# Sequence table scaled ahead of W1's issues and rounded behind them, and a last product in two column halves, in a fused attention, Fourier mixing and MLP kernel

## The chip, the cores and the metric

The kernel runs on one core of a Trainium2 chip. The metric is device time of one execution in microseconds (us); lower is better. The engines are named as in the profile: PE is TensorE, DVE is VectorE, ACT is ScalarE, POOL is GpSimd, SP is SyncE.

## The reference

Shapes: `q`, `k`, `v` are (8, 12, 448, 64), `w_ch1` is (768, 3072), `w_ch2` is (3072, 768), all float32; the output is (8, 448, 768).

```
scores = (q @ k.T) / sqrt(64);  attn = relu(scores)**2 / 448
x  = heads merged (attn @ v)                        # (8, 448, 768)
u  = x + real(fft(fft(x, over the sequence), over the channels))
un = (u - mean(u)) / sqrt(var(u) + 1e-6)            # over the channels
out = u + relu(un @ w_ch1) @ w_ch2
```

## The kernel before

**Work and stages.** Eight batches are taken one after the other. In a batch, four groups of three heads give scores on PE (L954), relu on ACT (L967), the square on DVE (L984) and the product with v on PE (L822, L827); its result, x transposed, is copied into `xT` (L671, L673, L689). The Fourier transform is two products with cosine and sine tables: over the channels (L1407, its result copied as `pc` by L1451), then over the 448 sequence positions (L1029), where x itself is added through an identity or a reversing matrix (L1032). Rows are normalised and turned (L1130, L1146), and two MLP products follow with weights that stay in on-chip memory; most of the MLP is formed on sums and differences of blocks (`Pair`), so that fewer products are needed.

**The first batch is special.** Its attention runs while the tables are still being made. Symmetric channels are first added and subtracted (`fold`, L748), on DVE, between the squares. The sequence table `seq` is made by `seq_table` on GpSimd: index numbers (L358, L360), scaled to turns in two pieces (L363, L366), rounded by adding and taking off 1.5*2^23 (L369), and the rounded part taken off (L371). Then `seq_sines` takes an absolute value on DVE (L377) and three sines on ACT (L383). Behind these ACT loads another function table (L399) and copies its half of `pc` (L1451); DVE copies the other half. The first batch's row products are eight: `rows(t, hf)` for four tiles t of 112 or 128 rows and two halves hf of 384 columns (L1029, L1032); the tiles 0 to 2 take banks of the pool `psS`, and `rows(3, 0)` and `rows(3, 1)` take one bank each of `psF`, a pool of two. Transposes of the next batch's q and k (`turn_on_pe`, L623) also take a bank of `psF`, which comes free when ACT or DVE has copied it into `qkT` (L630).

**What sets the order.** Everything is written as generators. Each step of one says `yield need(engine, duration, dependencies, banks)`, and a planner (`Streams.run`) picks at compile time, with these estimated durations, the step that could start first; equal ones go by a rank that `sch.add(generator, rank)` gives, lower first. So each engine's order is fixed in the program, an engine does its instructions strictly in that order, and a changed estimate or rank can move instructions anywhere. GpSimd issues the loads, in the order of the generator `loading`: `load_group(i, which, parts)` loads q (0), k (1) or v (2) of group i, `parts` 0 being the first 384 positions and 1 the last 64 (`load_halves`, L451); `load_w1` issues six pieces of W1 (L515); `mirrors`, called inside `load_group(NG + 1, ...)`, builds the reversing matrices and the index lists.

**The end.** The last product of the last pair (`Pair.chain_a`, its last step) is 12 matmuls into a 128x384 tile (L2060); DVE adds it to the residual `o` (L1616), and SP stores `o` (L1596).

Of the kernel before, what the change touches and what calls it, by code (L numbers as in the profile page):

```python
# [161 lines left out]
def dve(n):  # L162
    return n / 960 + 0.15
# [14 lines left out]
def kernel(  # L178
# [174 lines left out]
    def seq_table():  # L353

        f = work.tile([128, 4 * KH], FP32, name="dfty", tag="uA", bufs=1)
        g = work.tile([128, 4 * KH], FP32, name="dfty", tag="uB", bufs=1)
        yield need("POOL", 0.55)
        nc.gpsimd.iota(drow[:, 0:2], pattern=[[128, 2]], base=0, channel_multiplier=1,  # L358
                       allow_small_or_imprecise_dtypes=True)
        nc.gpsimd.iota(dcol[:, 0:SX], pattern=[[1, SX]], base=0, channel_multiplier=0,  # L360
                       allow_small_or_imprecise_dtypes=True)
        yield need("POOL", 0.3)
        nc.gpsimd.tensor_scalar(drow[:, 0:2], drow[:, 0:2], 1.0 / S, None, op0=ALU.mult)  # L363
        for i in range(2):
            yield need("POOL", 0.45)
            nc.gpsimd.tensor_scalar(f[:, i * SX:(i + 1) * SX], dcol[:, 0:SX], drow[:, i:i + 1], None, op0=ALU.mult)  # L366
        f, g = f[:, 0:2 * SX], g[:, 0:2 * SX]
        yield need("POOL", 0.75)
        nc.gpsimd.tensor_scalar(g, f, ROUND, -ROUND, op0=ALU.add, op1=ALU.add)  # L369
        e = yield need("POOL", 1.1)  # L370
        nc.gpsimd.tensor_tensor(f, f, g, op=ALU.subtract)  # L371
        sch.add(seq_sines(f, g, e + LATENCY["POOL"]), (0, 0.3))

    def seq_sines(f, g, e):

# [7 lines left out]
            nc.scalar.activation(dst, y, AF.Sin, bias=bias, scale=sign * 2.0 * math.pi)  # L383
        seq_ready.t = nseq_ready.t = dft_ready.t = e + LATENCY["ACT"]

    ROUND = 1.5 * 2 ** 23
    chan_made, dft_made = [Cell() for _ in range(3)], Cell()

# [67 lines left out]
    def load_group(i, which=(0, 1, 2), parts=(0, 1)):  # L456

        b, g = divmod(i, NG)
        hs = slice(g * HG, (g + 1) * HG)
        for x, src in enumerate((q, k, v)):  # L460
            if x not in which:
                continue
            if 0 in parts:
                if b == 0 and x < 2:
                    e = yield need("POOL", 0.75, ring())
                    t = first_qk[x][:R, g] if x == 0 else first_qk[x][:, g]
                else:
# [8 lines left out]
                nc.gpsimd.dma_start(out=to, in_=src[b, hs, 0:rows].rearrange("h (p j) d -> p h (j d)", j=j))  # L476
                loads[i][x] = None if x == 2 else t.rearrange("p h (j d) -> p j h d", j=4)
                landed.append(sch.dma(e, GRP * rows / S, 390e3, "sw"))
                arrive(i, x)
            if i == 0 and x == 1:  # L480
                e = yield need("POOL", 0.55)
                dft_indices()
                indices_ready.t = e + LATENCY["POOL"]
                yield need("POOL", 0.6)
                make_identity(nc, ident)
            if x and 1 in parts and (b > 0 or g == x - 1):
                yield from load_halves(b, g if b else 0, 1 if b else NG, x)
            if i == 2 and x == 2:
                yield need("POOL", 0.75)
                pads()  # L490
            if i == NG + 1 and x == 1 and 0 in parts:
                yield need("POOL", 3.6)
                mirrors()


    qk_left = Cell()
# [35 lines left out]
    def loading():  # L532
        for i in range(NG):
            yield from load_group(i)

        yield from load_group(NG, (0, 1))
        yield from load_group(NG + 1, (0, 1), (0,))
        yield from load_w1(0)
        yield from seq_table()
        yield from load_group(NG + 1, (1,), (1,))  # L540
        yield from load_w1(1)
        for i in (NG, NG + 1):
            yield from load_group(i, (2,), (0,))
# [1010 lines left out]
    def uses():  # L1554
# [11 lines left out]
                at += [(g, c, 0, 0), (g, c + 1, 0, 1 + odd), (g, c + 1, 1, 3 + odd), (g, c, 1, 5)]  # L1566
        return at

    os, ot, added = {}, {}, {}
    for g, c, hf, _ in uses():  # L1570
        ot[g, c, hf], added[g, c, hf] = Cell(), Cell()

    def outputs(slot):

        for g, c, hf, at in uses():
# [19 lines left out]
            e = yield need("SP", 0.1, [added[g, c, hf]])  # L1595
            nc.sync.dma_start(out=rows[t0:t0 + 128, cs], in_=o)  # L1596
            e = sch.dma(e, 128 * DH * 4)
            yield need("SP", 0.0, [e])

    def ffns():  # L1600
# [6 lines left out]
    def adder(b, NC, pool):  # L1607
# [4 lines left out]
        def add(pc, e, c, hf, give=True):  # L1612

            e = yield need("DVE", dve(DH), [e + LATENCY["PE"], ot[b, c, hf]])
            o = os[b, c, hf]
            nc.vector.tensor_tensor(o, pc[:, 0:DH], o, op=ALU.add)  # L1616
            if give:
                pool.give(pc, e)
            left[c, hf] -= 1
# [388 lines left out]
    class Pair:  # L2008
# [4 lines left out]
        def __init__(self, b, c, at, ht, add, advance, pieces, pool):  # L2013
# [3 lines left out]
            self.r12, self.r4 = ([Cell() for _ in pieces] for _ in range(2))  # L2017
            self.m1, self.m2, self.done = Cell(), Cell(), [Cell(), Cell()]
            self.reads = Cell(), Cell()
            self.waits, Pair.read = Pair.read, [self.reads[0], self.reads[1], *self.r4]  # L2020

        def early(self):
# [34 lines left out]
        def product(self, pc, lhs, rhs, start, i0=0, i1=KP):  # L2057

            for i in range(i0, i1):
                nc.tensor.matmul(pc[:, 0:DH], lhsT=lhs[i], rhs=rhs[i], start=(start and i == 0),  # L2060
                                 stop=(i == KP - 1), skip_group_check=True)
            self.advance((i1 - i0) * mm(DH))

        def first(self, k):

# [21 lines left out]
        def chain_a(self):  # L2087
# [111 lines left out]
```

## Time and profile before

| | |
|---|---|
| Runs | 571.01, 571.33, 572.6 us; median 571.33 us |
| Profiled execution | 570.35 us, of which the span from first to last instruction is 568.2 us |
| Granted TensorE clock | 1.000 |
| Busy | PE 557.6 us (98%), DVE 440.4 us (78%), ACT 317.3 us (56%), POOL 202.4 us (36%) |
| Chain that ended last | PE 92%, DVE 3%, ACT 2%, POOL 1%, DMA 1% |
| DMA | 82.43 MB, 145 GB/s over the span |

All times inside the kernel are microseconds from the start of this execution's span. The tables for the first batch are made in the first 37 us; the first batch's row products stand at 36.7 to 43.7 us, its turned rows at 43.5 to 47 us, and from there PE has work queued nearly to the end.

### The profile page before, as it was taken

The numbers are of one execution on the slowest core, as the hardware profiler recorded it, in microseconds if no ns is written. First come the engines' busy times: TensorE is split into PE (matmuls) and PEld (weight loads), VectorE is DVE, ScalarE is ACT, GpSimd is POOL, SyncE is SP. The second block draws the span as 40 slices with busy tenths as digits, with TensorE's granted clock in tenths as the row PEclk, the third lists the DMA queues.
The fourth block names the chain that finished last, engine by engine and source line by source line (L and its number), as shares of the span: only waits on it lengthen the run. The fifth ranks groups of instructions, "written<-read, shape, count | busy, mean of one in ns | idle before, by whom it ended". The sixth has DMA issues, their size and how long they took to land.

```text
span 568.2 us, 11250 instructions
## 1 busy us (share of the span) xinstructions
PE 557.6 (98%) x4223; PEld 352.2 (62%) x4228; DVE 440.4 (78%) x1018; ACT 317.3 (56%) x530; POOL 202.4 (36%) x284
## 2 busy tenths in 40 slices
PE   8989999999999999999999999999999999999997
PEld 6456546644355555546756756757678688668864
DVE  6977675887788977887998897888799957644762
ACT  5967873667645677676786647728515164005400
POOL 8986325514345234463545535325006000000000
PEclk9999999999999999999999999999999999999999
DMA  9999999989968989899699989957425431232012
GB/s 112 170 197 235 190 220 184 245 126 114 186 87 218 221 125 170 150 191 212 155 158 182 217 128 195 162 119 172 103 66 157 115 99 21 77 114 69 1 55 85
DMA packets 152545, 82.43 MB, mean 145 GB/s; under 512 B 118060, under 2 KB 147756, under 8 KB 152492
## 3 DMA queue, kind: packets, MB, share of 16 engines
q0 software_dynamic: 57056, 33.63, 42.8%
q1 hardware_dynamic: 95436, 48.09, 37.4%
q8 instruction: 33, 0.54, 0.4%
q14 instruction: 20, 0.16, 0.1%
HBM read 62.91 MB, written 26.25 MB: 157 GB/s over the span
## 4 chain that ended last, share of the span: by engine, by line
PE 92%; DVE 3%; ACT 2%; DMA 1%; POOL 1%; issue 1%; POOLq 0%; DVEq 0%; ACTq 0%
PE psF L1920 27%; PE psF L2060 21%; PE psS L1752 8%; PE psS L954 7%; PE psS L2060 5%; PE psF L827 5%; PE psF L1975 4%; PE psF L1948 4%; PE psS L1432 2%; PE psF L1752 2%; PE psF L822 1%; DMA qk<-in_k_dram 1%; DVE sq L984 1%; PE psS L827 1%; PE psS L1029 1%; ACT sq L967 1%
## 5 line engine op out<-in xcount | busy, mean ns | idle before, releaser
L1920 PE MATMUL psF<-unT,w 128*128 128x256 bf16 (+2 forms) x1147 | 165.0, 299 | 1.3 <-DVE hT L1905 0.9
L967 ACT ACTIVATE sq<-psS 128x896 bf16<-128x896 f32 x168 | 144.3, 920 | 32.1 <-PE psS L954 31.6
L1920 PEld LDWEIGHTS <-w 128*128 128x128 bf16 x1152 | 110.8, 98 | 51.2 <-issue 6.9
L984 DVE TENSOR_TENSOR sq<-sq 128x896 bf16<-128x896 bf16 x143 | 88.9, 639 | 12.0 <-ACT sq L967 11.3
L2060 PEld LDWEIGHTS <-hT 128*128 128x128 bf16 x648 | 62.5, 98 | 43.6 <-issue 3.9
L1907 ACT ACTIVATE hT<-psF 128x512 bf16<-128x512 f32 (+2 forms) x118 | 57.9, 507 | 42.3 <-PE psF L1920 41.6
L1616 DVE TENSOR_TENSOR o<-psF,o 128x384 f32<-128x384 f32 x77 | 42.6, 553 | 25.5 <-PE psF L2060 19.8
L2060 PE MATMUL psF<-w,hT 128*128 128x384 bf16 x336 | 60.1, 326 | 0.7 <-DVE o L1616 0.6
L954 PE MATMUL psS<-qkT 64*128 64x448 bf16 (+1 forms) x336 | 51.6, 355 | 1.1 <-ACT sq L967 0.6
L1767 ACT COPY copies<-psS 128x256 f32<-128x256 f32 x57 | 19.9, 374 | 53.9 <-PE psS L1752 48.7
L1275 POOL TENSOR_TENSOR u<-tp,xn 112x385 f32<-112x385 f32 (+2 forms) x14 | 14.5, 1039 | 83.6 <-DVE tp L1255 64.1
L689 DVE TENSOR_SCALAR xT<-psF 128x224 bf16<-128x224 f32 x62 | 21.2, 384 | 24.7 <-PE psF L827 24.7
L476 POOL DMA_DIRECT2D qn<-in_q_dram x21 | 15.7, 748 | 59.0 <-DVE qkr L583 52.3
L954 PEld LDWEIGHTS <-qkT 64*128 64x128 bf16 (+1 forms) x336 | 13.0, 94 | 32.7 <-issue 27.6
L827 PE MATMUL psF<-sq,vn 128*64 128x448 bf16 x246 | 32.6, 362 | 0.0
L1752 PEld LDWEIGHTS <-w 128*128 128x128 bf16 x288 | 28.2, 98 | 4.7 <-issue 1.1
L451 POOL DMA_DIRECT2D vn<-in_v_dram x42 | 26.1, 638 | 8.7 <-DMA w<-in_moe_w_ch_dram 7.4
L451 POOL DMA_DIRECT2D kn<-in_k_dram x42 | 25.7, 624 | 9.3 <-DMA w<-in_moe_w_ch_dram 6.3
L476 POOL DMA_DIRECT2D vn<-in_v_dram x24 | 19.1, 798 | 27.7 <-PE psS L954 27.4
L1284 DVE BATCH_NORM_STATS2 stats<-u 112x6 f32<-112x384 f32 (+2 forms) x56 | 28.5, 542 | 0.0
L1303 ACT ACTIVATE un<-u,small 113x768 bf16<-113x768 f32 (+2 forms) x21 | 20.9, 1024 | 11.8 <-DVE small L1290 9.2
L1772 DVE CUSTOM_DVE_ANT_0 hT<-psS,copies 128x256 bf16<-128x256 f32 x37 | 15.0, 421 | 14.1 <-PE psS L1752 6.2
(238 smaller groups left out, 961.6 us busy)
## 6 DMA issues: line engine op xcount, KB each, us to landing
out_dram<-o SPq DMA_DIRECT2D x56, 192.0 KB, 2.7
qn<-in_q_dram POOLq DMA_DIRECT2D x21, 224.0 KB, 5.0
vn<-in_v_dram POOLq DMA_DIRECT2D x24, 192.0 KB, 5.3
w<-in_moe_w_ch_dram POOLq DMA_DIRECT2D x12, 384.0 KB, 8.7
w<-in_moe_w_ch_dram POOLq DMA_DIRECT2D x4, 1152.0 KB, 19.7
kn<-in_k_dram POOLq DMA_DIRECT2D x21, 192.0 KB, 6.1
utop<-u SPq DMA_DIRECT2D x12, 336.0 KB, 3.1
o<-utop SPq DMA_DIRECT2D x16, 192.0 KB, 4.3
```

The source lines that it names most:

```text
L451: nc.gpsimd.dma_start(out=t[par * Dh:(par + 1) * Dh, par::2], in_=at)
L476: nc.gpsimd.dma_start(out=to, in_=src[b, hs, 0:rows].rearrange("h (p j) d -> p h (j d)", j=j))
L827: nc.tensor.matmul(av[h * Dh:(h + 1) * Dh, 0:S], lhsT=vn_home[:, at:at + Dh], rhs=sq[:, h, :], start=start, stop=stop, skip_group_check=True)
L954: nc.tensor.matmul(sc[:, h, 0:S].rearrange("k (c q) -> k c q", c=4), lhsT=flat[ps, k0:k0 + KB], rhs=qT[ps, pair], start=True, stop=True)
L967: nc.scalar.activation(r, sc[:, :, 0:S], AF.Relu)
L984: nc.vector.tensor_tensor(r, r, r, op=ALU.mult)
L1284: nc.vector.bn_stats(stats[:n, hf, :], u[:n, hf * (D // 2):(hf + 1) * (D // 2)])
L1616: nc.vector.tensor_tensor(o, pc[:, 0:DH], o, op=ALU.add)
L1752: nc.tensor.matmul(ps[:, 0:N], lhsT=lhs, rhs=rhs[:, m], start=(start and m == 0), stop=(stop and m == 2), skip_group_check=True)
L1907: nc.scalar.activation(hs, ps, AF.Relu)
L1920: nc.tensor.matmul(ph[:, i * N:(i + 1) * N], lhsT=w1_sb[m][hf][:, (jj + i) * 128:(jj + i + 1) * 128], rhs=unT[:, m, 0:N], start=(m == 0), ...
L2060: nc.tensor.matmul(pc[:, 0:DH], lhsT=lhs[i], rhs=rhs[i], start=(start and i == 0), stop=(i == KP - 1), skip_group_check=True)
```

## The change

It does four things. (1) `seq_table` is cut in two: index numbers and scaling stay in `seq_table`, which GpSimd now runs ahead of `load_w1(0)`, and the two rounding steps become `seq_rounds`, run behind it. (2) `mirrors` moves from inside `load_group(NG + 1, ...)` to behind `seq_rounds`, and the last 64 positions of k for group NG (two DMAs), which were loaded ahead, move behind `mirrors`. (3) The planner is given other durations for GpSimd's steps and a lower rank (-1, 0) for `seq_sines`. (4) The last product is written as two halves of 192 columns, each with its own add and its own store.

```diff
 def seq_table():
     ...
-        yield need("POOL", 0.3)
+        yield need("POOL", 0.6)
         nc.gpsimd.tensor_scalar(drow[:, 0:2], drow[:, 0:2], 1.0 / S, None, op0=ALU.mult)
         for i in range(2):
-            yield need("POOL", 0.45)
+            yield need("POOL", 1.3)
             nc.gpsimd.tensor_scalar(f[:, i * SX:(i + 1) * SX], dcol[:, 0:SX], drow[:, i:i + 1], None, op0=ALU.mult)
-        f, g = f[:, 0:2 * SX], g[:, 0:2 * SX]
-        yield need("POOL", 0.75)
+        seq_turns.append((f[:, 0:2 * SX], g[:, 0:2 * SX]))
+
+    def seq_rounds():
+        f, g = seq_turns.pop()
+        yield need("POOL", 1.85)
         nc.gpsimd.tensor_scalar(g, f, ROUND, -ROUND, op0=ALU.add, op1=ALU.add)
-        e = yield need("POOL", 1.1)
+        e = yield need("POOL", 1.5)
         nc.gpsimd.tensor_tensor(f, f, g, op=ALU.subtract)
-        sch.add(seq_sines(f, g, e + LATENCY["POOL"]), (0, 0.3))
+        sch.add(seq_sines(f, g, e + LATENCY["POOL"]), (-1, 0))
 ...
 def load_group(...):
-            if i == NG + 1 and x == 1 and 0 in parts:
-                yield need("POOL", 3.6)
-                mirrors()
 ...
 def loading():
-        yield from load_group(NG, (0, 1))
+        yield from load_group(NG, (0, 1), (0,))
         yield from load_group(NG + 1, (0, 1), (0,))
+        yield from seq_table()
         yield from load_w1(0)
-        yield from seq_table()
+        yield from seq_rounds()
+        yield need("POOL", 3.2)
+        mirrors()
+        yield from load_group(NG, (1,), (1,))
         yield from load_group(NG + 1, (1,), (1,))
         yield from load_w1(1)
 ...                                              # the store of the last tile
+            parts = [(slice(0, DH), added[g, c, hf])]
+            if (g, c, hf) == LAST:
+                parts = [(slice(0, DH // 2), half_added), (slice(DH // 2, DH), added[g, c, hf])]
+            for p, a in parts:
+                e = yield need("SP", 0.1, [a])
+                nc.sync.dma_start(out=rows[t0:t0 + 128, hf * DH + p.start:hf * DH + p.stop], in_=o[:, p])
 ...                                              # the last product
-            e = yield need("PE", d, [t] + self.r4)
-            self.product(pc, self.block(1, self.L), self.weights(1, 1), False)
-            self.done[0].t = e
-            yield from self.add(pc, e, c, 1)
+            for cols in self.parts:
+                n = cols.stop - cols.start
+                e = yield need("PE", KP * mm(n), [t] + self.r4)
+                self.product(pc, self.block(1, self.L), self.weights(1, 1), False, cols=cols)
+                self.done[0].t = e
+                if n < DH:
+                    sch.add(self.add(pc, e, c, 1, cols.stop == DH, cols), (0, 0))
+                else:
+                    yield from self.add(pc, e, c, 1)
```

In the changed file the lines around these places have higher numbers: L369 and L371 become L373 and L375, L377 becomes L381, L623 and L630 become L629 and L636, L748 becomes L754, L984 becomes L990, L1029 becomes L1035, L1081 becomes L1087, L1146 becomes L1152, L1451 becomes L1457, L1596 and L1616 become L1607 and L1627, L2060 becomes L2075.

The program's order shows where instructions went. On GpSimd, before, the twelve rows from the end of `mirrors` (`order`) over W1's six issues (`w_0` to `w_5`) to the rounding of the table (`dfty`):

```order
L303 TENSOR_SCALAR order<-order 128x1
L515 DMA w_0_0_531<-in_moe_w_ch_dram 128x1536
L515 DMA w_1_0_540<-in_moe_w_ch_dram 128x1536
L515 DMA w_2_0_554<-in_moe_w_ch_dram 128x1536
L515 DMA w_3_0_564<-in_moe_w_ch_dram 128x1536
L515 DMA w_4_0_571<-in_moe_w_ch_dram 128x1536
L515 DMA w_5_0_581<-in_moe_w_ch_dram 128x1536
L358 IOTA drow 128x2
L360 IOTA early 128x240
L363 TENSOR_SCALAR drow<-drow 128x2
L366 TENSOR_SCALAR dfty<-early,drow 128x240 x2
L369 TENSOR_SCALAR dfty<-dfty 128x480
```

And after, from the index numbers to the start of `mirrors` (`rev`):

```order
L358 IOTA drow 128x2
L360 IOTA early 128x240
L363 TENSOR_SCALAR drow<-drow 128x2
L366 TENSOR_SCALAR dfty<-early,drow 128x240 x2
L517 DMA w_0_0_493<-in_moe_w_ch_dram 128x1536
L517 DMA w_1_0_508<-in_moe_w_ch_dram 128x1536
L517 DMA w_2_0_516<-in_moe_w_ch_dram 128x1536
L517 DMA w_3_0_526<-in_moe_w_ch_dram 128x1536
L517 DMA w_4_0_539<-in_moe_w_ch_dram 128x1536
L517 DMA w_5_0_549<-in_moe_w_ch_dram 128x1536
L373 TENSOR_SCALAR dfty<-dfty 128x480
L375 TENSOR_TENSOR dfty<-dfty 128x480
```

The five scaling steps now stand ahead of W1's issues, and the two rounding steps follow them at once, where `mirrors` used to stand ahead of all.

On PE, around the start of the last of the first batch's eight row products, `rows(3, 1)`. Before, its first matmul (`seqm`) follows the end of `rows(3, 0)` and waits for nothing of its own:

```order
L1032 LDWEIGHTS xT_107
L1032 MATMUL psF<-ident,xT_107 112x128
L1029 LDWEIGHTS seqm
L1029 MATMUL psF<-pc,seqm 112x384
L1029 LDWEIGHTS seqm
L1029 MATMUL psF<-pc,seqm 112x384
```

After, transposes of the next batch's k (`kn`) stand ahead of it, and it waits for a semaphore of ACT:

```order
L629 LDWEIGHTS kn [waits DMASW7_49]
L629 MATMUL psF<-ident,kn 64x128
L629 LDWEIGHTS kn [waits DMASW0_49]
L629 MATMUL psF<-ident,kn 64x128
L1035 LDWEIGHTS seqm
L1035 MATMUL psF<-pc,seqm 112x384 [waits Activation_49]
```

The eight k transposes moved from ahead of all row products to here, and the wait is for ACT's copy into `qkT` (L636), which gives back the bank of `psF` that these transposes filled.

On ACT, that copy itself. Before, it stands right behind ACT's half of `pc` and ahead of every copy of a row product (`u`):

```order
L1451 CAST pc<-psS 128x2x193 [waits PE_49]
L1451 CAST pc<-psS 128x2x193
L630 COPY qkT<-psF 128x960 [waits PE_49]
L1081 COPY u<-psS 128x384 [waits DVE_49,Activation_49]
L1065 ACTIVATE small<-small,few 128x1 [waits DVE_49]
```

After, it stands behind the last of them that reads `psS`, right ahead of the copy of the turned rows (`unT`):

```order
L1087 COPY u<-psS 112x384 [waits DVE_49]
L1071 ACTIVATE small<-small,few 112x1 [waits DVE_49]
L1087 COPY u<-psS 112x384 [waits PE_49]
L636 COPY qkT<-psF 128x960 [waits PE_49]
L1152 CAST unT<-psS 128x6x128 [waits DMASW2_49,DMASW5_49,DMASW0_49,PE_49]
```

So the copy moved past all of ACT's copies of the row products of tiles 0 to 2, and PE's last row product, which waits for its bank, stands behind it. On DVE, the absolute value (L377, after L381) moved from among the last folds to ahead of the first fold, right behind five squares. At the end, the 12 matmuls of 384 columns became 24 of 192, and one add and one store became two of each.

More of the change, by code (lines that the diff above doesn't have):

```diff
@@ L384, in seq_sines @@
         seq_ready.t = nseq_ready.t = dft_ready.t = e + LATENCY["ACT"]
+    seq_turns = []
     ROUND = 1.5 * 2 ** 23
@@ L1567, in uses @@
         return at
+    LAST, half_added = (NGR - 1, 0, 1), Cell()
     os, ot, added = {}, {}, {}
@@ L1594, in outputs @@
             ot[g, c, hf].t = sch.dma(e, 128 * DH * 4)
-            e = yield need("SP", 0.1, [added[g, c, hf]])
-            nc.sync.dma_start(out=rows[t0:t0 + 128, cs], in_=o)
-            e = sch.dma(e, 128 * DH * 4)
+            parts = [(slice(0, DH), added[g, c, hf])]
[4 more added lines that the diff above has]
+                nc.sync.dma_start(out=rows[t0:t0 + 128, hf * DH + p.start:hf * DH + p.stop], in_=o[:, p])
+                e = sch.dma(e, 128 * (p.stop - p.start) * 4)
             yield need("SP", 0.0, [e])
@@ L1610, in adder, with add @@
                 for c in range(NC) for hf in range(2)}
-        def add(pc, e, c, hf, give=True):
-            e = yield need("DVE", dve(DH), [e + LATENCY["PE"], ot[b, c, hf]])
+        def add(pc, e, c, hf, give=True, cols=slice(0, DH)):
+            e = yield need("DVE", dve(cols.stop - cols.start), [e + LATENCY["PE"], ot[b, c, hf]])
             o = os[b, c, hf]
-            nc.vector.tensor_tensor(o, pc[:, 0:DH], o, op=ALU.add)
+            nc.vector.tensor_tensor(o[:, cols], pc[:, cols], o[:, cols], op=ALU.add)
             if give:
                 pool.give(pc, e)
+            if cols.stop < DH:
+                half_added.t = e + LATENCY["DVE"]
+                return
             left[c, hf] -= 1
@@ L2019, in __init__ @@
             self.reads = Cell(), Cell()
+            self.parts = [slice(0, DH // 2), slice(DH // 2, DH)] if (b, c, 1) == LAST else [slice(0, DH)]
             self.waits, Pair.read = Pair.read, [self.reads[0], self.reads[1], *self.r4]
@@ L2055, in sums, with product @@
             return made[n][k][:, i0 - CH[k][0]:i1 - CH[k][0]]
-        def product(self, pc, lhs, rhs, start, i0=0, i1=KP):
+        def product(self, pc, lhs, rhs, start, i0=0, i1=KP, cols=slice(0, DH)):
             for i in range(i0, i1):
-                nc.tensor.matmul(pc[:, 0:DH], lhsT=lhs[i], rhs=rhs[i], start=(start and i == 0),
+                nc.tensor.matmul(pc[:, cols], lhsT=lhs[i], rhs=rhs[i][:, cols], start=(start and i == 0),
                                  stop=(i == KP - 1), skip_group_check=True)
-            self.advance((i1 - i0) * mm(DH))
+            self.advance((i1 - i0) * mm(cols.stop - cols.start))
         def first(self, k):
```

## The prediction

> **What bounds the kernel now.** I read the page's totals first, then the chain of waits, then the timelines of the engines that the chain names in the first 45 us.
>
> ```profile
> span 568.2 us, 11250 instructions
> PE 557.6 (98%) x4223; PEld 352.2 (62%) x4228; DVE 440.4 (78%) x1018; ACT 317.3 (56%) x530; POOL 202.4 (36%) x284
> PE 92%; DVE 3%; ACT 2%; DMA 1%; POOL 1%; issue 1%; POOLq 0%; DVEq 0%; ACTq 0%
> ```
>
> PE is 98% busy and 92% of the chain. The change takes no PE work away, so it can only shorten the few stretches where PE has nothing to do, or the tail behind its last matmul. The chain from 31 to 45 us, its pieces in order of time (start, length, what), shows the one such stretch that the change touches:
>
> ```profile
> 32.67 1.28 ACT seqm L383 x2
> 34.55 1.28 ACT L399
> 36.14 0.49 ACT pc L1451
> 36.67 0.94 PE psS L1029 x4
> 43.68 0.35 PE psS L1130 x6
> 44.05 0.80 ACT unT L1146
> ```
>
> PE waits until 36.67 for `pc`, ACT's copy, which stands behind the sequence table's sines (L383) and a table load (L399). The sines wait for the table, and the table for GpSimd. Behind that come eight row products (L1029, L1032) and the turned rows (L1130, L1146). GpSimd, DVE and ACT in that stretch (start, length, engine, line):
>
> ```profile
> 15.38 1.22 POOL L451 DMA_DIRECT2D kn<-in_k_dram  x2
> 17.28 0.80 POOL L476 DMA_DIRECT2D kn<-in_k_dram  x1
> 21.40 3.37 POOL L515 DMA_DIRECT2D w<-in_moe_w_ch_dram  x6
> 24.74 0.20 POOL L358 IOTA drow<- 128x2 f32 x1
> 26.04 2.65 POOL L366 TENSOR_SCALAR dfty<-early,drow 128x240 f32<-128x240 f32 x2
> 28.77 1.84 POOL L369 TENSOR_SCALAR dfty<-dfty 128x480 f32<-128x480 f32 x1
> 30.70 1.48 POOL L371 TENSOR_TENSOR dfty<-dfty 128x480 f32<-128x480 f32 x1
> ```
> ```profile
> 22.16 1.69 DVE L984 TENSOR_TENSOR sq<-sq 128x896 bf16<-128x896 bf16 x3
> 24.09 0.69 DVE L673 TENSOR_SCALAR xT<-psF 128x224 bf16<-128x224 f32 x2 [0.23 <-PE psF L822]
> 24.69 2.94 DVE L984 TENSOR_TENSOR sq<-sq 128x896 bf16<-128x896 bf16 x5
> 27.56 0.82 DVE L748 TENSOR_TENSOR fold<-xT 128x225 bf16<-128x225 bf16 x3
> 28.84 0.65 DVE L748 TENSOR_TENSOR fold<-xT 128x225 bf16<-128x225 bf16 x1
> 29.41 0.61 DVE L984 TENSOR_TENSOR sq<-sq 128x896 bf16<-128x896 bf16 x1
> 29.95 0.64 DVE L748 TENSOR_TENSOR fold<-xT 128x225 bf16<-128x225 bf16 x3
> 31.04 1.28 DVE L748 TENSOR_TENSOR fold<-xT 128x225 bf16<-128x225 bf16 x1
> 33.64 0.46 DVE L748 TENSOR_TENSOR fold<-xT 128x225 bf16<-128x225 bf16 x2
> 34.88 1.07 DVE L1451 CAST pc<-psS 97x386 bf16<-97x386 f32 x2 [0.77 <-PE psS L1407]
> ```
> ```profile
> 28.91 0.99 ACT L967 ACTIVATE sq<-psS 128x896 bf16<-128x896 f32 x1
> 36.05 1.03 ACT L1451 CAST pc<-psS 128x386 bf16<-128x386 f32 x2
> 36.92 0.96 ACT L630 COPY qkT<-psF 128x960 bf16<-128x960 bf16 x1
> 43.10 0.46 ACT L1081 COPY u<-psS 112x384 f32<-112x384 f32 x1
> ```
>
> DVE is full from 24.69 on, so what it loses there counts. One fold costs 0.28 us (three take 0.64, two 0.46: a step of 0.18), yet the one at 28.84 took 0.65, beside GpSimd's rounding, and the one at 31.04 took 1.28 and ended as GpSimd's subtraction did (30.70 + 1.48 = 32.18). They lost 0.37 and 1.00. The folds at 27.56 lost 0.82 - 0.64 = 0.18 beside the scaling. Three squares take 1.69, so five take 2.76; the five at 24.69 lost 0.18. In all GpSimd costs DVE 1.73 us here.
>
> **Part 1, the table on GpSimd.** The two small loads of k (1.22) leave the place ahead of the q and k loads, which then end at 17.28 + 0.80 - 1.22 = 16.9. Index numbers and scaling take from 24.74 to 26.04 + 2.65 = 28.69, so 3.95; they now end at 20.8. W1's six issues take 3.37: 24.2. The rounding steps, 1.84 and 1.48 with gaps, end at about 27.7 instead of 32.18, 4.5 us earlier. `mirrors` (18.08 to 21.40: 3.3) then runs to 31.0, and four small loads of k at 0.61 to 33.4. Before, W1's second half could start at 32.18 + 1.22 = 33.4: the same, so no weight comes later, and W1's first half is issued 0.6 earlier. The small loads of k are needed by transposes at about 41 us, 9 us after their issue, against this:
>
> ```profile
> kn<-in_k_dram POOLq DMA_DIRECT2D x21, 192.0 KB, 6.1
> ```
>
> I cost them at nothing; if a queue of W1 pieces held them 3 us longer, PE would wait by so much.
>
> **Part 2, DVE and ACT.** The scaling's 0.36 of loss moves to 17 to 21 us, where DVE's later idle of 0.23 (at 24.09) takes up most: 0.13 stays. The rounding's 1.37 moves from the folds to the five squares, which end at 27.63 - 0.18 + 1.37 + 0.13 = 28.95. The absolute value comes right behind them, so the table is no longer waited for. The last fold ends at 34.10 - 1.73 + 1.50 = 33.87, and DVE's part of `pc` at 35.95 - 0.23 = 35.72. On ACT the last relu (L967) ended at 29.90, 2.27 behind the fifth square; by that lag it now ends at 31.2, and the sines start there instead of at 32.67. From the first sine to `pc` it is 36.14 - 32.67 = 3.47: ACT's `pc` starts at 34.7 and its two pieces (1.03) end at 35.7, like DVE's. Before, the last piece of `pc` came at 36.05 + 1.03 = 37.08. So the row products gain G = 1.4 us. If the rounding cost the squares nothing, G would be 1.4 + 1.5 = 2.9; a loss of 1 us more than taken gives 0.4.
>
> **Part 3, what takes it back.** The order shows ACT's copy L630 moved from ahead of the row products' copies to behind those of tiles 0 to 2, and PE's `rows(3, 1)` waiting for it, since both take a bank of the pool of two. PE began `rows(3, 1)` at 42.69:
>
> ```profile
> 42.69 0.49 PE L1029 MATMUL psF<-pc,seqm 128*112 128x384 bf16 x2
> ```
>
> ACT's last copy of tile 2 ended at 43.10 + 0.46 = 43.56, itself behind row products that move by G. L630 takes 0.96, of which 0.1 overlaps: it ends at 44.4 - G, and `rows(3, 1)` starts there instead of at 42.69. The shift of all that follows is 1.7 - G: +0.3 for G = 1.4, -1.2 for 2.9, +1.3 for 0.4. Queued behind the waiting matmul on PE are the turned rows (L1130), for which ACT's `unT` waits. The eight k transposes that moved to this place lie inside the wait. The bank held by the copy is the one resource that the trace of before never shows short; if its wait did not bind, the shift would be -G.
>
> **Part 4, the end.**
>
> ```profile
> 562.87 1.96 PE psF L2060 x12
> 564.85 0.56 DVE o L1616
> L1616 DVE TENSOR_TENSOR o<-psF,o 128x384 f32<-128x384 f32 x77 | 42.6, 553 | 25.5 <-PE psF L2060 19.8
> L689 DVE TENSOR_SCALAR xT<-psF 128x224 bf16<-128x224 f32 x62 | 21.2, 384 | 24.7 <-PE psF L827 24.7
> 90.17 2.00 PE psS L1432 x24
> DMA to landing us min/median/max: 1.9/1.9/1.9
> out_dram<-o SPq DMA_DIRECT2D x56, 192.0 KB, 2.7
> utop<-u SPq DMA_DIRECT2D x12, 336.0 KB, 3.1
> ```
>
> Twelve matmuls of 384 columns become 24 of 192: 24 of 193 took 2.00 against 1.96, +0.04. The first half's add and store run beside the second half's matmuls. The last add has 192 columns: 384 took 553 ns and 224 columns 384 ns, 1.06 ns a column, so 0.35 us, -0.2. The last store has 96 KB instead of 192; the one of before landed in 1.9. Between none and half of that goes (0 to -0.95). The two SP rows give 0.4 us for 144 KB more, so 0.27 for 96 KB: I take -0.25. The end brings -0.4, with bounds of -0.15 and -1.1.
>
> **Sum.** +0.3 - 0.4 = -0.1: the profiled execution goes from 570.35 to 570.25. The median of the runs shown, 571.33, lies 1.0 higher, so the median becomes 571.2. With G from 0.5 to 2.3 (front +1.2 to -0.6) and the end from -0.15 to -0.8, this case runs from 569.9 to 572.4.
>
> **Rivals.** *A, the forecast:* the front's gain is taken back by the wait on the moved copy; 571.2; chance 0.66. For it speaks that the wait stands in the order and that its price is a copy of 0.96 on an engine that goes strictly in order.
>
> *B, the gain stays:* the squares hardly feel the rounding, or the wait does not bind. For it, the square at 29.41 took 0.61 in the middle of the rounding (28.77 to 30.61), and the five squares at 24.69 lost only 0.18 beside the scaling. Against it, the subtraction did stop a fold by 1.00. Front -1.2 to -1.4, end -0.4: -1.7, so 569.6; chance 0.20. That the end brings nothing is inside A and B.
>
> *C, slower:* the rounding stops DVE for its whole length. It sits beside the folds now and beside back-to-back squares after. If the two steps hold the squares for 1.84 + 1.48 = 3.32 instead of 1.37, all of DVE, and ACT's relus and sines behind it, come 1.95 later: `pc` at 37.67, G = -0.6, front +2.3, total +1.9: 573.2. It decides from a loss of about 3.2 us up. The subtraction's row (a fold that ends as it does) speaks for it, the square of 0.61 beside the rounding against it; chance 0.14.
>
> The Trainium skill ("SBUF — State Buffer", section "Who interferes with whom", and its section on the two separate sides) has the port pair shared by VectorE and GpSimd as an exclusive lock, which whoever starts first holds for the whole instruction; a VectorE operation with two on-chip inputs meets it against a GpSimd operation that reads on-chip memory. Squares and folds are such operations, so by that rule C would be the outcome, 573.2. The trace agrees for the subtraction (1.28 for a fold) and not for the rounding (0.61 for a square that began inside it), and the measurement decides.
>
> **How the numbers follow.** A difference of 0.3%, 1.7 us, is about what a measurement of this kernel can tell from no change. A lies within it but for its ends; B lies at its edge, mostly outside; C is outside. Faster by more: 0.15 of B and 0.05 of A, 0.20. Slower by more: 0.12 of C and 0.03 of A, 0.15. The same: 0.65. The range holds A and reaches into B and C until some 0.2 are left out: 569.5 to 573.0.
>
> **What would show it.** In the profile of the changed kernel: the subtraction (L375) ending near 27.7 and the absolute value (L381) right behind the fifth square near 29; the five squares at 4.1 to 4.3 us instead of 2.94 (2.8 speaks for B, over 5.5 for C); the last piece of `pc` near 35.7; ACT's copy L636 directly ahead of `unT`; PE idle ahead of `rows(3, 1)`, released by ACT, and that product starting near 43.0; the last add at 0.35 and the last landing near 1.65. PE's total of busy time should stay at 557.6 within 0.5. The forecast is wrong if `rows(3, 1)` starts before 42 or after 44.5, or if a wait for a small load of k shows ahead of the transposes.

## The result, and the profile after

The changed kernel took 573.31 us in the median of 22 runs (571.81 to 575.87), the kernel before 570.79 in 22 runs beside it (570.10 to 576.42): the ratio is 1.0037, with a 95% interval from 1.0022 to 1.0052. The change makes the kernel slower by about 2.1 us; forecast was 571.2, within 0.3% of no change. Half of before's runs (11 of these 22) lie within 0.6 us of its lowest, and 2 of after's 22 within 0.6 us of after's. The profiled execution took 573.05 us against 570.35 (+2.70), its span 570.9 against 568.2.

The page of after, its totals and its chain by engine:

```profile
span 570.9 us, 11280 instructions
PE 558.0 (98%) x4240; PEld 353.5 (62%) x4240; DVE 439.3 (77%) x1019; ACT 317.5 (56%) x530; POOL 201.6 (35%) x284
PE 78%; DMA 10%; POOL 7%; DVE 2%; issue 1%; ACT 1%; POOLq 0%; DVEq 0%; ACTq 0%
```

PE's busy time is the same within 0.4, so what is new is waiting. The chain had 92% of PE and 1% each of DMA and POOL; now DMA has 10% and POOL 7%. That is the first sign of a loss that the prediction doesn't have: GpSimd and transfers have come onto the path.

If each PE instruction of after is set beside the same one of before, the differences show where the time went: -1.37 at the first row product (36.67 to 35.31), +0.61 at `rows(3, 1)`, still +0.60 at 103 us, +1.93 at 105 us, +2.18 from 315 us on, and 2.7 at the end of the span. So +0.6 from the front, +1.3 at 105 us, +0.2 at about 300 us, and +0.5 behind the last matmuls.

**The front.** GpSimd, DVE, ACT and PE of after in the timelines (start, length, engine, line, how many; in brackets the idle time before and what ended it):

```profile
22.76 2.06 POOL L373 TENSOR_SCALAR dfty<-dfty 128x480 f32<-128x480 f32 x1
24.91 1.33 POOL L375 TENSOR_TENSOR dfty<-dfty 128x480 f32<-128x480 f32 x1
```
```profile
21.97 2.07 DVE L990 TENSOR_TENSOR sq<-sq 128x896 bf16<-128x896 bf16 x3
24.57 3.85 DVE L990 TENSOR_TENSOR sq<-sq 128x896 bf16<-128x896 bf16 x5
28.34 0.40 DVE L381 TENSOR_SCALAR dfty<-dfty 128x480 int32<-128x480 int32 x1
33.18 0.46 DVE L754 TENSOR_TENSOR fold<-xT 128x225 bf16<-128x225 bf16 x2
34.99 1.06 DVE L1457 CAST pc<-psS 97x386 bf16<-97x386 f32 x2 [1.35 <-PE psS L1413]
```
```profile
34.66 1.05 ACT L1457 CAST pc<-psS 128x386 bf16<-128x386 f32 x2 [1.04 <-PE psS L1413]
41.92 0.46 ACT L1087 COPY u<-psS 112x384 f32<-112x384 f32 x1
42.28 0.96 ACT L636 COPY qkT<-psF 128x960 bf16<-128x960 bf16 x1
```
```profile
43.30 0.49 PE L1035 MATMUL psF<-pc,seqm 128*112 128x384 bf16 x2 [1.28 <-ACT qkT L636]
```

The table is ready at 26.2 us. The squares pay for it: three beside the rounding take 2.07 instead of 1.69, five beside the subtraction 3.85 instead of 2.76, together 1.47. One by one in the trace, the square that begins inside the subtraction (at 25.10) takes 1.62 instead of 0.62, and the one inside the rounding (at 23.04) takes 1.00. The absolute value stands right behind them at 28.34. The folds end at 33.64, half a microsecond earlier than before, but both engines' copies of `pc` now wait for PE (L1413): its products run one behind the other from 32.3 and end at 34.95, where before they ended at 34.84. The last row is the wait on the moved copy: PE idle 1.28, released by ACT's L636.

**At 105 us.** Here the turned rows of the second batch (L1211, L1205 before) stand on PE. GpSimd, ACT and PE before:

```profile
90.06 0.72 POOL L476 DMA_DIRECT2D qn<-in_q_dram  x1 [6.78 <-DMA w<-in_moe_w_ch_dram]
91.94 0.75 POOL L476 DMA_DIRECT2D kn<-in_k_dram  x1 [1.17 <-DMA qn<-in_q_dram]
92.70 1.20 POOL L451 DMA_DIRECT2D kn<-in_k_dram  x2
98.74 0.99 POOL L1275 TENSOR_TENSOR u<-tp,xn 128x385 f32<-128x385 f32 x1
103.17 1.95 ACT L1303 ACTIVATE un<-u,small 128x768 bf16<-128x768 f32 x2 [1.47 <-DVE small L1290]
105.04 0.50 PE L1205 MATMUL psS<-ident,un 128*128 128x128 bf16 x6
```

And after:

```profile
91.86 0.72 POOL L481 DMA_DIRECT2D qn<-in_q_dram  x1 [5.39 <-DMA w<-in_moe_w_ch_dram]
94.22 0.76 POOL L481 DMA_DIRECT2D kn<-in_k_dram  x1 [1.64 <-DMA qn<-in_q_dram]
96.22 1.19 POOL L456 DMA_DIRECT2D kn<-in_k_dram  x2 [1.24 <-DMA kn<-in_k_dram]
101.83 0.60 POOL L456 DMA_DIRECT2D kn<-in_k_dram  x1 [0.39 <-DMA kn<-in_k_dram]
102.44 0.93 POOL L1281 TENSOR_TENSOR u<-tp,xn 128x385 f32<-128x385 f32 x1
105.89 1.95 ACT L1309 ACTIVATE un<-u,small 128x768 bf16<-128x768 f32 x2 [0.55 <-DVE small L1296]
106.97 0.51 PE L1211 MATMUL psS<-ident,un 128*128 128x128 bf16 x6 [1.18 <-ACT un L1309]
```

GpSimd makes half of the second batch's residual sums, four additions (L1275 and L1277; L1281 and L1283 after). In its order these additions stand behind eleven loads, and a load waits until the transfer eight loads earlier has landed (in both traces, `qn` for a piece of W2, the next `kn` for a `qn`, each eight issues back in GpSimd's order). After, a piece of W2 (`w`) lands 1.8 us later (91.86 against 90.06), and behind it three loads wait (1.64, 1.24 and 0.39 us) where two did before (1.17 and 0.27): 102.44 - 98.74 = 3.7 us later for the additions. ACT's `un` follows, and PE waits 1.18 us. Before, it waited for nothing there: ACT's first `un` was done at 104.20, 0.84 ahead of PE's turned rows.

**The end.** DVE's last adds:

```profile
567.06 0.62 DVE L1627 TENSOR_TENSOR o<-psF,o 128x192 f32<-128x192 f32 x2 [1.42 <-PE psF L2075]
```

PE's 24 matmuls ran from 564.88 to 567.02. Both adds stand behind the last of them: the first half's add has not run beside the second half. Two adds take 0.62 where one took 0.56, and the two stores are issued one behind the other; still the last store lands 2.52 us behind the last matmul, where before it was 2.49. The half microsecond comes later: from that landing to the end of the span it is 1.35 us instead of 0.91. SP ends the program with a row of waits on its semaphores, in a fixed order, 0.06 us each. Before, the last store's semaphore stood last in that row; after, it stands third, and seven waits follow it.

### The profile page after: what moved, and what is told of

Its sections match the earlier page's. It is cut to its first block, busy times and chain, and to the rows that moved or that the text cites. A ratio compares the mean times of both kernels' runs of the same rounds, so it can differ in the third digit from the quotient of the medians.

```text
span 570.9 us, 11280 instructions
## 1 busy us (share of the span) xinstructions
PE 558.0 (98%) x4240; PEld 353.5 (62%) x4240; DVE 439.3 (77%) x1019; ACT 317.5 (56%) x530; POOL 201.6 (35%) x284
## 4 chain that ended last, share of the span: by engine, by line
PE 78%; DMA 10%; POOL 7%; DVE 2%; issue 1%; ACT 1%; POOLq 0%; DVEq 0%; ACTq 0%
PE psF L1934 23%; PE psF L2075 20%; PE psS L1766 8%; PE psS L960 6%; DMA kn<-in_k_dram 5%; PE psS L2075 5%; PE psF L1989 4%; PE psF L833 3%; DMA vn<-in_v_dram 3%; PE psS L1438 2%; DMA w<-in_moe_w_ch_dram 2%; PE psF L1766 2%; PE psF L1962 2%; POOL w L517 1%; PE psF L828 1%
## 5 line engine op out<-in xcount | busy, mean ns | idle before, releaser
L990 DVE TENSOR_TENSOR sq<-sq 128x896 bf16<-128x896 bf16 x143 | 89.9, 645 | 11.5 <-ACT sq L973 10.7
L2075 PEld LDWEIGHTS <-hT 128*128 128x128 bf16 x648 | 62.7, 98 | 43.5 <-issue 4.0
L1627 DVE TENSOR_TENSOR o<-psF,o 128x384 f32<-128x384 f32 (+1 forms) x78 | 42.5, 546 | 24.1 <-PE psF L2075 20.5
L2075 PE MATMUL psF<-w,hT 128*128 128x384 bf16 x336 | 59.9, 326 | 0.6 <-DVE o L1627 0.6
L1281 POOL TENSOR_TENSOR u<-tp,xn 112x385 f32<-112x385 f32 (+2 forms) x14 | 15.1, 1075 | 81.7 <-DVE tp L1261 62.3
L1293 ACT ACTIVATE small<-small,few 112x1 f32<-112x1 f32 (+2 forms) x28 | 8.2, 298 | 32.0 <-DVE small L1291 28.9
```

What stands on the lines that cost most here:

```text
L990: nc.vector.tensor_tensor(r, r, r, op=ALU.mult)
L1627: nc.vector.tensor_tensor(o[:, cols], pc[:, cols], o[:, cols], op=ALU.add)
L2075: nc.tensor.matmul(pc[:, cols], lhsT=lhs[i], rhs=rhs[i][:, cols], start=(start and i == 0), stop=(i == KP - 1), skip_group_check=True)
```

## The experiments

**The halves alone.** Before, with the edit of the last product:

```diff
+            for cols in self.parts:          # two halves of 192 columns, as in after
+                ...
+                sch.add(self.add(pc, e, c, 1, cols.stop == DH, cols), (0, 0))
```

> Before with only the last product's two halves (two adds, two stores). Theory A (the prediction): the first half's add runs beside the second half's matmuls, the last add and store are half as large: 0.4 us faster than before. Theory B (the bank): both halves lie in one tile of one bank, so the first add waits for the last matmul of both; then nothing runs beside anything, there are two adds and two store issues behind the last matmul, and the end takes about 0.5 us more than before. The front is that of before in both, PE's rows(3,1) at 42.7.

Measured: 571.22 us against 571.03, ratio 1.0009 (0.9988 to 1.0029); its lowest run is 570.88 against 570.75. In the trace the two adds stand behind the last matmul as in after. The forecast gain of 0.4 is not there. The span of the fastest run is 0.5 longer (569.1 against 568.6), as the second theory has it, but the time is only 0.13 longer, because 1.7 to 1.8 us lie outside the span in each of its runs and 2.1 to 2.2 in each of before's. After has 2.1 to 2.2 there too, so that its 0.5 counts in full; why the kernels differ in this is not shown.

Two more things stand in this profile. PE waits at 105 us as in after (1.59 us), though nothing ahead of the last product was edited. And its lateness does not come from the row products: `rows(3, 1)` was on time (within 0.05), and at 50 us DVE's copy into `qkT` (L630) began 0.6 late, after which PE is 0.59 late. So the wait is not new with the change. This execution took 572.91, one of five that took 572.8 or more; the other seven lie within 0.4 us of the lowest.

A difference of the same kind is seen with the front of after, below: 570.07 with the halves (lowest 569.69), 569.79 without (lowest 569.16).

**The halves in two banks.** The second half gets a bank of its own; what the earlier products left in its columns is added to `o` ahead:

```diff
+            nc.vector.tensor_tensor(o[:, cols], pc[:, cols], o[:, cols], op=ALU.add)   # earlier products' columns 192..383
...
+                if own:
+                    pc = self.pool.take(e)
+                self.product(pc, self.block(1, self.L), self.weights(1, 1), own, cols=cols)
```

> Before with the last product's two halves in two banks: what the first three products left in the second half's columns is added to the residual by one more DVE add of 192 columns beside other PE work, and the second half's matmuls start a bank of their own. If the bank shared by both halves held the first add back, that add now starts about 1.0 us ahead of the last matmul's end, and behind that stand only one add of 0.35 and one store of 96 KB: 0.3 to 0.4 us below before. If two adds and two stores cost by themselves whatever stands beside them, the time is 0.2 us above before, as with the halves in one bank.

DVE at the end of that kernel:

```profile
564.18 0.36 DVE L1621 TENSOR_TENSOR o<-psF,o 128x192 f32<-128x192 f32 x1 [0.43 <-PE psF L2069]
565.17 0.36 DVE L1621 TENSOR_TENSOR o<-psS,o 128x192 f32<-128x192 f32 x1 [0.63 <-PE psS L2069]
```

The first add now starts a microsecond ahead of the second, beside PE's matmuls, and the last store lands 1.6 us behind its issue instead of 1.9. In its trace PE raises the semaphore that DVE waits for after each half (564.16 and 565.15), in after's once, behind the last of the 24 matmuls (567.04). So what held the add was a dependency of the program, which both halves shared with their tile and its bank; which of the two it goes by was not tested. The time is 570.38 against 570.90, ratio 0.9989 (0.9972 to 1.0005): not told apart from no change. In the trace the last store lands 2.05 us behind the last matmul instead of 2.49, but from that landing to the end of the span it is 1.35 us instead of 0.91, with seven of SP's closing semaphore waits, 0.06 each, behind it where before had none. The fastest runs have the same span (568.0); what the time gains lies outside the span (1.8 to 1.9 us against 2.1 to 2.2).

**The moved copy alone.** Before, with only the two small loads of k put behind the table:

```diff
-        yield from load_group(NG, (0, 1))
+        yield from load_group(NG, (0, 1), (0,))
...
+        yield from load_group(NG, (1,), (1,))          # behind seq_table
```

> Before, with one thing of the change: the last 64 positions of k for the next batch's first group are loaded behind the table instead of with the group, which moves ACT's copy into qkT behind the row products' copies. The table is made as before. The wait on the copy: rows(3,1) starts at about 44.4 instead of 42.7, so 1.7 us later. Lateness theory for the wait at 105 us: a front 1.7 us late gives that wait too, so 3 us or more above before in all. Load order theory: 1.7 us above before and no more.

```profile
43.97 0.49 PE L1030 MATMUL psF<-pc,seqm 128*112 128x384 bf16 x2 [1.28 <-ACT qkT L631]
```

The wait of 1.28 appears with nothing else of the change, and `rows(3, 1)` starts 1.28 later than before (1.7 was expected; the row products began 0.5 earlier in this execution). At 105 us PE loses another 1.4, 2.7 in all. In the median 572.79 against 571.03, ratio 1.0021 (1.0003 to 1.0039); the 3 us of the lateness theory are not reached.

**Two that left the plan.** The same loads put back into the changed kernel, and a longer estimate for the planner:

```diff
+        yield from load_group(NG, (0, 1))              # first kernel: as in before
...
-        return [landed[-8] + 1.2] if len(landed) > 7 else []
+        return [landed[-8] + 4.0] if len(landed) > 7 else []     # second kernel
```

> After, but with the last 64 positions of k for the next batch's first group loaded with the group, as before; ACT's copy into qkT is then back ahead of the row products' copies, and rows(3,1) waits for nothing of ACT's. All else of the change stays, the halves too. If the moved copy takes the table's gain away: rows(3,1) starts at 41.3 instead of 43.3 (2 us earlier than after). For PE's new wait at 105 us there are two theories. Lateness: it grows out of a front that is 0.6 us late, so it goes, and the time is about 1.4 - 0.5 = 0.9 us below before. Load order: it comes from the table and the loads on GpSimd in another order, so it stays, and the time is about 0.4 us above before.

> After, but the planner's estimate of how long a load on GpSimd waits for a transfer eight loads earlier is 4.0 instead of 1.2 us behind that transfer's landing; this puts GpSimd's four additions of the second batch (L1281, L1283) ahead of the loads of k that they stand behind. If PE's wait at 105 us comes from additions that stand behind waiting loads in GpSimd's order, that wait (1.3 us) goes, and the time is 1.3 us below after. If it comes from elsewhere (DVE, ACT, or the turned rows' own inputs), it stays as it is. rows(3,1) starts at 43.3 as in after.

Measured: 587.46 us (ratio 1.0247, 1.0205 to 1.0288) and 580.47 (1.0155, 1.0116 to 1.0195). Neither tells the theories apart, and the first expectation's "all else" did not hold: the planner drew other orders to the end of the program. Set beside after in the traces, PE's order of some 8,500 rows differs in 2,600 and 3,000 lines, where the kernel with the small loads moved alone differs from before in 40. What they show is how much one estimate is worth in this planner. The next kernels therefore leave every step of the planner as it is and move only where an instruction is written out.

**The copy put back by hand.** After, with the k transposes and ACT's copy written where before has them:

```diff
+                ahead = (b, g, r) == (1, 0, 0)
+                for z in ((0, 1) if x == 0 else ()) if ahead else (x,):     # k's transposes with q's
...
+        while turned_ahead:                                                # first_tail, ahead of the row products
+            turned_ahead.pop()()                                           # ACT's copy
```

> After, with the eight k transposes and ACT's copy into qkT put back to where they stand in before (ahead of the row products); every other instruction of every engine, the loads' order and the halves at the end stay as in after. If the wait on that copy is what takes the table's gain back, PE begins its last row product at about 41.5 instead of 43.3 (1.2 us ahead of before). For the new wait of PE at 105 us: the lateness theory says that it goes with the lateness, so the time is about 1.2 less 0.3 = 0.9 us below before; the load order theory says that it stays (1.3 us), so the time is about 0.4 us above before.

```profile
42.29 0.49 PE L1042 MATMUL psF<-pc,seqm 128*112 128x384 bf16 x2
```

`rows(3, 1)` started at 42.29, with no wait, although this execution's row products began only 0.46 earlier than before (its first 20 us ran late). PE stays 0.40 ahead of before to 290 us, and the wait at 105 us isn't there. Median 570.07 against 570.90; the ratio of 1.0003 (0.9977 to 1.0028) can't tell it from before.

**Lateness alone.** Before, with four more matmuls ahead of `rows(3, 1)`:

```diff
+            for _ in range(4 if t == 3 and hf == 1 else 0):
+                nc.tensor.matmul(pu[:n, 0:D // 2], ..., start=True, stop=True)
```

> Before, with four more matmuls of 384 columns on PE ahead of the last row product of the first batch (their result is overwritten); nothing else moves on any engine. They cost PE 4 x 0.165 = 0.66 us at 42.7 us. Lateness theory: that alone brings the wait at 105 us in most executions, so the time is 0.66 + 1.3 = about 2.0 us above before. Load order theory: 0.66 us above before and no more, and PE's turned rows at 105 us come 0.66 late.

```profile
92.26 0.72 POOL L476 DMA_DIRECT2D qn<-in_q_dram  x1 [6.07 <-DMA w<-in_moe_w_ch_dram]
102.77 0.93 POOL L1279 TENSOR_TENSOR u<-tp,xn 128x385 f32<-128x385 f32 x1
107.30 0.51 PE L1209 MATMUL psS<-ident,un 128*128 128x128 bf16 x6 [1.69 <-ACT un L1307]
```

No load was moved, and yet the W2 piece lands 2.2 us later than in before and PE waits 1.69 at the same place. The median is 572.34 against 570.90, but the ratio of 1.0014 (1.0002 to 1.0026) is 0.8 us, with 0.1 to 1.5 as its interval, which can't tell 0.66 from the 2.0 of the lateness theory; and the halves alone had this wait without it. What speaks for lateness is how the runs lie. Within 0.6 us of their own lowest run are 2 of 11 here, 2 of 22 of after and 2 of 12 of the moved copy alone, the three kernels whose row products are made late; of before it is 55 of 109 in the four sets of runs that it has on record, and of the copy put back 7 of 12. So with a late front nearly all runs lie 0.6 us or more above their kernel's best, where half of before's do. No execution of before with a wait at 105 us was profiled, so it is likely, and not shown, that its other half loses there too.

**The front without its losses.** The copy put back and the last product whole:

> The table's new place and order as in after, k transposes and ACT's copy where before has them, and the last product whole as in before. If the two losses are the copy (with the wait that follows from lateness) and the end, this keeps the table's gain alone: rows(3,1) at about 41.5, 1.2 us below before in all. If GpSimd's other order costs something of its own further on, it is less, and PE's shift against before grows behind 44 us.

Median 569.79 against 570.90, ratio 0.9982 (0.9971 to 0.9993); the lowest run is 569.16. Half of its runs (6 of 12) lie within 0.6 us of that, the others 1.1 to 2.1 above. The profiled execution is one of the others: PE was 1.17 ahead up to 103 us and lost 1.83 at 105 us.

```profile
105.70 0.51 PE L1220 MATMUL psS<-ident,un 128*128 128x128 bf16 x6 [1.67 <-ACT un L1318]
```

So a late front isn't needed for that wait: the loads can wait for transfers here too.

**The additions ahead of the loads.** Four loads of q and k on GpSimd are written out behind the four additions, in after and in the kernel just shown:

```diff
+                (held_loads.append if i == 2 * NG + 2 and x < 2 else lambda f: f())(load)
...
+            while (b, ch, i) == (1, 1, 1) and held_loads:      # behind the fourth addition
+                held_loads.pop(0)()
```

> After, with GpSimd's four additions of the second batch ahead of the four loads of q and k that they stand behind; nothing else moves on any engine. If PE's wait at 105 us comes from those additions standing behind loads that wait for transfers, they start about 3 us earlier (99 to 100 us instead of 102.4), PE's wait goes and the time falls by about 1.3 us, to 571.8 where before has its usual 570.1 to 570.8. If it comes from anything else, the time stays 2.5 us above before.

GpSimd and PE of after with this one move:

```profile
92.95 0.72 POOL L484 DMA_DIRECT2D qn<-in_q_dram  x1 [6.86 <-DMA w<-in_moe_w_ch_dram]
100.08 1.72 POOL L1285 TENSOR_TENSOR u<-tp,xn 128x385 f32<-128x385 f32 x1
107.07 0.50 PE L1215 MATMUL psS<-ident,un 128*128 128x128 bf16 x6
```

This execution was 2.0 us late at the front and the W2 piece landed later than in any other. Still PE doesn't wait at 105 us: its lateness is 2.03 at 55 us and 2.03 at 535 us. Median 571.66 against 571.98, ratio 0.9996 (0.9975 to 1.0017): the lowest run is 0.6 us above that of before, where after's was 1.7 above. Seven of its twelve runs lie within 0.6 us of the lowest, where 2 of 22 of after did. The larger part of after's loss is gone with this move.

> The table's new place, k transposes and ACT's copy as in before, the last product whole, and the four additions ahead of the four loads. The front's gain of 1.2 us should then stay in every execution and not in half of them: median at about 569.2 where before's usual time is 570.1, and fewer executions a microsecond or two above it. If the wait at 105 us has another source, it keeps the two groups of times of the kernel without this move.

Median 569.83 against 571.98, ratio 0.9966 (0.9945 to 0.9988); ten of twelve runs lie within 0.6 us of the lowest, 569.74, where 13 of 29 of before do. This version beats before, and after with it; the front without its losses does so too. Their two ratios can't be set against each other, since before's median was 571.98 in this set of runs and 570.90 in that one; the medians are the same (569.83 and 569.79), and what the move changes is how many runs lie over 0.6 us above the lowest (2 of 12 instead of 6).

> The same with the last product's halves in two banks. If the banks were what held the halves back, this is 0.2 to 0.4 us below the kernel with the last product whole; if the additional add and store eat that, it is equal or up to 0.2 us above it.

Median 570.13 against 571.98, ratio 0.9970 (0.9956 to 0.9985): the halves in two banks add nothing to it that shows.

One profiled execution of each kernel but the two that left the plan, with PE's lateness against before at about 83 us ("front"), the start of GpSimd's load that waits for the W2 piece, the start of the additions, and PE's wait at 105 us:

| kernel | front | load starts | additions start | PE waits |
|---|---|---|---|---|
| before | 0 | 90.06 | 98.74 | 0 |
| front without its losses | -1.17 | 90.17 | 101.18 | 1.67 |
| copy put back | -0.40 | 89.57 | 98.05 | 0 |
| halves in two banks | -0.07 | 90.31 | 99.55 | 0 |
| lateness alone | +0.42 | 92.26 | 102.77 | 1.69 |
| halves alone | +0.59 | 91.67 | 102.86 | 1.59 |
| after | +0.60 | 91.86 | 102.44 | 1.18 |
| moved copy alone | +1.28 | 92.65 | 103.20 | 1.26 |
| after, additions ahead | +2.03 | 92.95 | 100.08 | 0 |
| the best, additions ahead | +0.66 | 90.63 | 97.06 | 0.05 |
| the best, halves in two banks | +0.09 | 89.39 | 96.14 | 0 |

PE waits wherever the additions start behind 101 us. All four fronts that were 0.4 to 1.3 us late, with the order of before on GpSimd here, have it; of the four that were not, one has it. Not every lateness in this table was made by an edit: in the halves alone and in the best kernel `rows(3, 1)` was within 0.05 of before, and DVE's copy into `qkT` at 50 us began 0.6 late. The best kernel's execution is also the slowest of its twelve (571.19), and PE still loses 0.2 us at 105 us in it.

## Why the prediction was wrong

**Where the 2.8 us between forecast and profile lie.** Forecast was -0.1 for the profiled execution, and it was +2.7: 0.3 at the front, 1.3 at 105 us, 0.2 at about 300 us and 0.9 at the end.

**Part 1 was right.** The roundings ended at 26.2 (27.7 forecast, since the scaling took 1.77 here and 2.65 before), no weight came later for it, and the small loads of k held nobody up.

**Part 2 was right in its terms, G a little too large.** The roundings cost DVE 1.47 (1.37 + 0.13 forecast), 0.38 for the first step and 1.09 for the second, as they cost the folds before (0.37 and 1.00). The last fold ended at 33.64 (33.87). ACT's half of `pc` ended at 35.71, as forecast, DVE's at 36.05 instead of 35.72, since PE's last products for it (L1413) could not follow the folds faster. Tile 2's last copy on ACT ended at 42.38 against 43.56 before, so G was 1.2 there, not 1.4.

**Part 3 named the right wait and priced it 0.3 low.** L636 ended at 43.24 and `rows(3, 1)` began at 43.30: +0.61 where +0.3 was forecast. The moved copy alone gives the same wait of 1.28, and with the copy put back it is gone: that rival A's mechanism holds is shown.

**Part 3 stopped at 44 us, and that was the failing step, the larger of two.** It let the front's shift run through unchanged "for all that follows". In fact something waited behind it with 0.84 us to spare: the turned rows at 105 us. The loads ahead of the additions already waited for transfers in the trace of before (6.78, 1.17, 0.27 us at 90 to 95 us in the timeline of GpSimd); that the additions stood behind them in the same order was there to be read. The shift of 0.6 became 1.9. That the additions' place behind the loads makes the wait is shown by moving them. That a late front makes a loss common is shown by how the runs of three kernels with late fronts lie, each with this wait in its profile; that it isn't the only way to it, by the halves alone and by the front without its losses. Why the W2 piece lands about 2 us later when the front is 0.4 to 1.3 us late was not shown: the piece was issued only 0.3 later (its pair of issues starts at 59.32 in after, 59.04 in before), and the transfers of this stretch share the DMA engines, which were at least 80% busy in each slice from 80 to 95 us before; no run took one of them away.

**Part 4 had the wrong sign, and that was the other failing step.** "The first half's add and store run beside the second half's matmuls" did not hold, since PE's signal for both halves stood behind the last matmul. So the last store landed no earlier, and the additional store left seven of SP's closing waits behind that landing, a term that the sum didn't have: -0.4 became about +0.5 in the profile. Two banks give the overlap and bring the landing 0.44 forward, and the same closing waits take it back.

The rest, 0.2 at about 300 us, is left open; the kernel with the halves in two banks, with the front of before, loses 0.3 at 268 us.

**The rivals.** C gave a size near the result (573.2), and that was luck, for its reason was wrong: the two roundings took 3.39 us and cost DVE 1.47, so they did not stop it for their whole length. The Trainium skill's rule of the exclusive lock ("SBUF — State Buffer", section "Who interferes with whom") holds here only in part, as in the trace of before: the square that began inside the subtraction ended 0.48 behind the subtraction's end, the one that began inside the rounding 0.8 ahead of the rounding's. B, that the gain stays, is what the front does once the copy and the additions stand where they belong.

## What to carry to other kernels

Follow a shift past the place of the change: look in the trace for the next engine that works in order behind waiting loads, and ask how much later its work may come before the bound engine waits. A gain on one engine can be handed back by a single copy that an automatic plan moves, so compare the orders row by row, and test such a cause by writing out one instruction elsewhere, with the plan held fixed. Splitting a last product can pay only if the halves don't share what the first reader waits for, and if the additional store costs nothing behind it.

## What the runs showed of the hardware

Three squares on DVE beside GpSimd's rounding lost 0.38 us and five beside its subtraction 1.09, in the same amounts in all six executions with the table's new place (2.07 and 3.85). Half a microsecond of lateness went with transfers that landed about two later: in the table the load that waits for the W2 piece starts at 89.4 to 90.3 us where PE was at most 0.1 late, and at 91.7 to 93.0 in five of the six executions whose front was 0.4 us or more late; the sixth, the best kernel's, has 90.6. What in the transfers answers to the lateness is not shown. The closing waits of SP on its semaphores took 0.06 us each, and seven of them stood behind the last landing where the store's semaphore wasn't the last of their row. The time of a run holds more than its span, and not by the same amount: 2.1 to 2.2 us in before, 1.7 to 1.8 in the halves alone, so a change of a few tenths has to be seen in both.
